# Second weight matrix fetched one load sooner, wider fillers, a counted instruction fetch, and the last product copied and stored by token halves

## The chip, the cores and the metric

The kernel runs on one core of one Trainium2 chip. A core has five engines that run side by side and meet at semaphores: TensorE (PE in the profile; its weight loads are shown apart as PEld), VectorE (DVE), ScalarE (ACT), GpSimd (POOL) and SyncE (SP), and 16 DMA engines that move data between HBM and the on-chip memory. TensorE writes its results to PSUM, which has eight banks of 128 x 512 float32; VectorE and ScalarE carry them from there to the on-chip memory SBUF. The metric is the device time of one execution in microseconds. Three runs of the kernel before took 301.09, 302.47 and 301.96 us, with a median of 301.96 us.

## The reference

Retention (attention with a decay in place of a softmax) for 8 batches, 8 heads, 576 positions and 64 features per head, then a feed-forward layer over all 4,608 tokens:

```python
scale = 1.0 / np.sqrt(64)
scores = scale * np.matmul(q, k.transpose(0, 1, 3, 2))
gamma = 1.0 - 2.0 ** (-5.0 - np.arange(H))
rel = pos[:, None] - pos[None, :]
Dmat = np.where(rel >= 0, gamma[:, None, None] ** rel[None, :, :], 0.0)
attn_out = np.matmul(scores * Dmat[None], v)
x = attn_out.transpose(0, 2, 1, 3).reshape(B * S, 512)
h = x @ w_in                 # 512 -> 2048
g = h * np.cos(h)
out = g @ w_out              # 2048 -> 512, float32
```

All inputs are float32; the kernel multiplies in bfloat16 and sums in float32.

## The kernel before, in words

**Retention by units.** A unit is (batch, g): g = 0 and 1 are the two blocks of 256 positions, g = 2 the remaining 64 positions of four batches together. `unit` (L468) loads k, q and v of a unit on SyncE (`load`, L457), and casts and scales them, k (`natk`) by a plain cast on GpSimd at L454, q and v (`qnat`, `natv`) by a multiplication with the decay tables at L496, also on GpSimd. For the first units k and q are transposed on TensorE (`tpe`, L509), for the later ones by a DMA (`txb`, L528). `scores` (L565) makes q·k on TensorE and the masked copy `pt` on VectorE (L599); the running state k·v is summed in the banks `st`; `outputs` (L637) makes pt·v plus state·q, and ScalarE copies the result to `xt`, the left operand of the feed-forward layer. All of these small products have line L563 in the profile.

**Feed-forward by tiles.** Nine tiles of 512 tokens. `mlp1` (L727) makes one 128-row slice of h with four matmuls (L737), ScalarE makes cos(h) (L745) and VectorE the product `gt` (L748). For the first tiles it is done by halves of 256 tokens. The second product of tile 0 is plain (`plain2`, L767: sixteen groups of four matmuls of 512 columns, L776; group `qd` needs quarter `qd` of `w_out`). Tiles 1 to 8 use a Winograd form with seven products of half size (`wino2`, L805, order P1, P2, P6, P5, P7, P3, P4; L862), whose sums of `gt` (`s`, L823 and L829) and of `w_out` (`tw`, `wsums`, L802) are made on VectorE. Products that go into the output are copied by ScalarE (`snap`), or added by VectorE (`comb`, L874), into `os`, and `store` (L753) writes `os` to HBM from SyncE. The last tile holds the 64-position ends of all batches, so its rows go out as two stores of 64 partitions each.

**What sets the order.** Every operation is a task with an estimated duration. `Graph.run` (L204) places the tasks one after the other, engine by engine, by due times (`prio`), free PSUM banks and its own estimate of when an operand is there; the order so found is then written out as a fixed instruction stream for each engine. Waits are semaphores; every engine executes its own stream strictly in order. The estimates matter through the order alone. Three of them are touched here: `dma_free` (L294), when a transfer gets the DMA engines; `FETCH` with `left` (L134, L208, L237, L280), a model of TensorE's instruction fetch, which comes in blocks of 256 instructions; and `count`, how many instructions a TensorE task has.

**Loads of the weights.** `load_w` (L715) issues the four quarters of a weight matrix on GpSimd's own queue with a cast to bfloat16; `graph` (L902) gates them: w_in waits for the load of k of unit (1,0), w_out (L940) for the load of v of unit (1,1). The loads of unit (2,0), on SyncE's queue, wait for quarter 1 of w_out (L943); SyncE's later loads stand behind them.

**Fillers.** Where the plan leaves TensorE idle for more than 400 ns before the bank of `self.wb` is given back, `emit` (L383) puts in matmuls of ones by ones, 128 columns each (L401), whose result nobody reads.

**The end.** In the last tile P3's sum is stored first, then P4: sixteen matmuls into one bank, one copy on ScalarE, two stores of 64 partitions by 2 x 256 columns.

## Time and profile before

| | |
|---|---|
| median of three runs | 301.96 us |
| the profiled execution: its own time / its span | 301.62 us / 299.9 us |
| TensorE busy | 285.2 us, 95% of the span |
| VectorE / ScalarE / GpSimd busy | 213.0 / 169.7 / 101.4 us |
| TensorE clock granted | 1.00 over the span |
| moved by DMA | 49.87 MB, mean 166 GB/s |
| instruction fetch (queue q8) | 30 packets, 0.49 MB |

The span runs from the first to the last instruction of the profiled execution; 1.7 us of its time lie outside. A row of the timeline has the start, the duration, the engine, the line, the operation, what it writes and reads, how many instructions are merged, and in brackets the idle time before it with what ended it. The duration of a merged row ends with the last instruction. "issue" stands for idle time in which the engine waited for no semaphore. The table by windows has, for each stretch, its length and each engine's busy time with the number of instructions, then the granted clock, the busy share of the DMA engines and their GB/s. A DMA instruction of SP or POOL is shown while it is being issued; its data land later.

### The profile page before, as it was taken

Reading aid. Unit: us, or ns where it says so; the run is one execution under the profiler, and the core shown is the slowest. Engines: PE = TensorE matmul, PEld = TensorE weight load, DVE = VectorE, ACT = ScalarE, POOL = GpSimd, SP = SyncE. Lnnn points to the kernel's source line nnn. Section 1 sums busy time; section 2 is a strip of 40 time slices with the busy share of each in tenths; the row PEclk is TensorE's granted clock in tenths of the full one; section 3 lists DMA queues with packets and bytes.
Section 4 is the critical chain, followed back from the end, with each engine's and each line's share of the span. In section 5 each row is a group of like instructions: output and inputs, shape, how many; then the busy total and the mean of one; then the engine's idle time right before and its main releaser. Section 6 shows DMA issues by size and latency. Waiting matters only on the chain.

```text
span 299.9 us, 9086 instructions
## 1 busy us (share of the span) xinstructions
PE 285.2 (95%) x3809; PEld 202.7 (68%) x3815; DVE 213.0 (71%) x379; ACT 169.7 (57%) x315; POOL 101.4 (34%) x125
## 2 busy tenths in 40 slices
PE   6789888999999999999999999999999999999994
PEld 6667665666788876766676667666766666666683
DVE  2776495659985889697868686959777666667721
ACT  5369876556667565645655565466565555545420
POOL 3821960665825614825363515172100000000000
PEclk9999999999999999999999999999999999999999
DMA  7999789999999799997999986892103000300115
GB/s 199 252 203 274 202 129 236 280 200 299 207 251 297 151 194 281 214 227 210 229 280 232 244 188 94 194 236 53 24 2 140 2 2 2 140 2 0 70 73 140
DMA packets 101640, 49.87 MB, mean 166 GB/s; under 512 B 43488, under 2 KB 97248, under 8 KB 101600
## 3 DMA queue, kind: packets, MB, share of 16 engines
q1 hardware_dynamic: 97376, 45.10, 63.6%
q0 software_dynamic: 4224, 4.19, 8.8%
q8 instruction: 30, 0.49, 0.7%
q14 instruction: 10, 0.08, 0.1%
HBM read 36.70 MB, written 9.44 MB: 154 GB/s over the span
## 4 chain that ended last, share of the span: by engine, by line
PE 78%; DMA 14%; POOL 5%; issue 1%; SPq 0%; ACT 0%; DVE 0%; DVEq 0%
PE bk L737 35%; PE bk L862 33%; DMA stgq<-in_q_dram 8%; PE bk L563 6%; DMA wout<-in_moe_w_out_dram 3%; DMA win<-in_moe_w_in_dram 3%; PE bk L776 2%; POOL qnat L496 2%; POOL natv L496 2%; PE st L563 1%; POOL natk L454 1%; SPq L463 0%; POOL win L717 0%; POOL wout L721 0%; DVE qnat L496 0%
## 5 line engine op out<-in xcount | busy, mean ns | idle before, releaser
L745 ACT ACTIVATE cb<-bk,cpi 128x256 bf16<-128x256 f32 (+1 forms) x192 | 108.3, 583 | 82.0 <-PE bk L737 79.9
L737 PE MATMUL bk<-xt,win 128*128 128x256 bf16 (+1 forms) x768 | 144.2, 326 | 1.0 <-DMA win<-in_moe_w_in_dram 0.7
L748 DVE TENSOR_TENSOR gt<-bk,cb 128x256 bf16<-128x256 f32 (+1 forms) x192 | 103.8, 555 | 54.9 <-ACT cb L745 47.8
L737 PEld LDWEIGHTS bk<-xt,win 128*128 128x128 bf16 x768 | 72.3, 98 | 39.7 <-DVE pt L599 1.4
L496 POOL TENSOR_TENSOR natv<-stgv,wv 128x512 bf16<-128x512 f32 x36 | 37.7, 1070 | 37.0 <-PE bk L563 20.6
L599 DVE TENSOR_TENSOR pt<-bk,tr 128x512 bf16<-128x512 f32 x68 | 42.7, 682 | 5.5 <-PE bk L563 5.4
L496 POOL TENSOR_TENSOR qnat<-stgq,wq 128x512 bf16<-128x512 f32 x32 | 35.0, 1112 | 15.9 <-DMA stgq<-in_q_dram 15.3
L454 POOL CAST natk<-stgk 128x512 bf16<-128x512 f32 x34 | 21.3, 653 | 55.8 <-DMA stgk<-in_k_dram 44.8
L862 PE MATMUL bk<-wout,gt 128*128 128x256 bf16 x256 | 32.7, 273 | 0.0
L862 PE MATMUL bk<-tw,s 128*128 128x256 bf16 x256 | 32.7, 273 | 0.0
L862 PE MATMUL bk<-wout,s 128*128 128x256 bf16 x256 | 32.4, 273 | 0.0
L862 PEld LDWEIGHTS bk<-tw,s 128*128 128x128 bf16 x256 | 24.9, 98 | 8.1
L862 PEld LDWEIGHTS bk<-wout,gt 128*128 128x128 bf16 x256 | 24.7, 98 | 6.4
L862 PEld LDWEIGHTS bk<-wout,s 128*128 128x128 bf16 x256 | 24.7, 98 | 6.1
L453 ACT ACTIVATE xt<-bk 128x512 bf16<-128x512 f32 x36 | 23.5, 728 | 0.5 <-PE bk L563 0.5
L874 DVE TENSOR_TENSOR os<-bk,sn 128x512 f32<-128x512 f32 x24 | 16.4, 683 | 10.4 <-PE bk L862 10.4
L453 ACT ACTIVATE sn<-bk 128x512 f32<-128x512 f32 x24 | 14.3, 597 | 13.8 <-PE bk L862 13.8
L862 PE MATMUL bk<-tw,gt 128*128 128x256 bf16 x128 | 16.4, 273 | 0.0
L776 PE MATMUL bk<-wout,gt 128*128 128x512 bf16 x58 | 15.3, 380 | 0.6 <-issue 0.3
L862 PEld LDWEIGHTS bk<-tw,gt 128*128 128x128 bf16 x128 | 12.5, 98 | 4.0
L829 DVE TENSOR_TENSOR s<-gt 128x1024 bf16<-128x1024 bf16 x16 | 12.8, 800 | 0.2
L563 PE MATMUL bk<-qt,kt 64*64 64x128 bf16 (+1 forms) x576 | 12.1, 217 | 0.4 <-ACT xt L453 0.4
(58 smaller groups left out, 187.7 us busy)
## 6 DMA issues: line engine op xcount, KB each, us to landing
stgk<-in_k_dram SPq DMA_DIRECT2D x16, 512.0 KB, 7.0
stgq<-in_q_dram SPq DMA_DIRECT2D x16, 512.0 KB, 6.9
stgv<-in_v_dram SPq DMA_DIRECT2D x16, 512.0 KB, 6.9
out_dram<-os SPq DMA_DIRECT2D x16, 512.0 KB, 3.3
win<-in_moe_w_in_dram POOLq DMA_DIRECT2D x4, 512.0 KB, 9.0
wout<-in_moe_w_out_dram POOLq DMA_DIRECT2D x4, 512.0 KB, 10.0
stgk<-in_k_dram SPq DMA_DIRECT2D x8, 128.0 KB, 3.4
stgq<-in_q_dram SPq DMA_DIRECT2D x8, 128.0 KB, 3.5
```

The costliest lines, as they stand in the source:

```text
L453: return self.one(eng, dur, lambda e: e.activation(dst(), src(), AF.Copy), r=r, w=w, **kw)
L454: return self.one(eng, dur, lambda e: e.tensor_copy(dst(), src()), r=r, w=w, port=True, **kw)
L496: self.one(eng, 610 if eng == "dve" else 1000, lambda e, out=out, inp=inp, tab=tab, col=col, hs=hs: e.tensor_tensor(out(), inp(), ap(tab, ...
L563: return lambda e: e.matmul(out(), lhs(), rhs(), start=start, stop=True, skip_group_check=True)
L599: self.one("dve", 610, lambda e, r=r, b=b, pt=pt: e.tensor_tensor(ap(self.at(pt), 1024, 0, 128, 512 * r, [64 * ny * ny, 8 // ny // ny], [1 ...
L737: inst = e.matmul(ap(self.at(bk), 512, 0, 128, 0, [1, n]), ap(self.WIN, 4 * DFF, 0, 128, c * DFF + 128 * f, [1, 128]), ap(self.at(xt), 204 ...
L745: self.one("act", 70 + n, lambda e: e.activation(ap(self.at(cb), TB, 0, 128, 0, [1, n]), ap(self.at(bk), 512, 0, 128, 0, [1, n]), AF.Sin, ...
L748: self.one("dve", 75 + n / 0.96, lambda e: e.tensor_tensor(ap(self.at(gt), NF * TB, 0, 128, f * TB + 256 * h0, [1, n]), ap(self.at(bk), 51 ...
L776: inst = e.matmul(self.at(bk).ap(), ap(self.at(gt), NF * TB, 0, 128, f * TB + 256 * half + 128 * tt, [1, 128]), ap(self.WOUT, NF * DM, 0, ...
L829: self.one("dve", 610, lambda e, i=i, q=q, x=x, y=y, op=op: e.tensor_tensor(sv(i, q), x(), y(), op), r=r, w=[(S_[i, q],)], port=True, name ...
L862: inst = e.matmul(ap(self.at(bank), 512, 0, 128, 256 * tt, [1, 256]), l(f, tt), rr(f), start=(first and f == 0 and tt == 0), stop=True, sk ...
L874: self.one("dve", 610, lambda e: e.tensor_tensor(view(h, c), ap(self.at(bank), 512, 0, 128, 0, [256, 2], [1, 256]), ap(self.at(sn[name]), ...
```

## The change

Five edits in one:

1. `graph`: the quarters of w_out are gated by the load of q of unit (1,1), not of v, which is the next one on SyncE's queue. On GpSimd the four issues now stand ahead of the two multiplications that make `qnat` of unit (1,1), where they stood behind them. The loads of unit (2,0) wait for quarter 2 of w_out, where they waited for quarter 1.
2. `warm`: a filler is one matmul of 512 columns in place of 128, and there are fewer of them: 24 where there were 103. The sixth place (one filler) is the last; the five fillers within the scores of unit (1,1) are gone.
3. The planner counts TensorE's instructions (8.4 for four matmuls, 16.4 for eight, fillers too) and asks for block k at instruction 128 + 256 k, which it expects 6,500 ns later, when instruction 443 + 256 k needs it. `dma_free` charges a GpSimd transfer 2,400 ns rather than 1,700 ns where the queue would be empty.
4. In the last tile bank A becomes two banks, one for each 128 tokens. P4's two tasks are by tokens (all eight slices of one half, then of the other) rather than by slices. Copies and sums from A come in two halves of 128 x 256.
5. The last store of 64 x 2 x 256 in two instructions becomes 64 x 256 in four, two after each half's copy, all on SyncE.

Since the order is planned, edits 1 and 3 also change it: the `tpe` of q of unit (1,1) now stand behind the outputs of unit (0,1); four groups of `plain2` (two with quarter 0, two with quarter 1) stand ahead of and between the two halves of the scores of unit (1,1), which come later; and VectorE has the first two weight sums (`tw`, from quarters 0 and 1) ahead of the `pt` copies of unit (1,1). The states of unit (2,0) on TensorE now have nineteen `mlp1` groups of tile 1 behind them, where sixteen stood behind them. From tile 2 on, a few tasks change places.

```diff
-    AHEAD, FETCH = 2000, 3000
+    AHEAD, FETCH = 2000, 6500
...
+    def fill(gap, seen):
+        return int(0.6 * (gap - 150) / 220 if seen else (gap - 300) / 430)
...
-                if e == "pe" and t.count > left[0]:
-                    s = max(s, left[1] - t.dur * left[0] / t.count)
+                if e == "pe" and t.count:
+                    k = (seen + t.count - 443) // 256
+                    if k >= 0 and 443 + 256 * k > seen and k in asked:
+                        s = max(s, asked[k] + self.FETCH - t.dur * (443 + 256 * k - seen) / t.count)
...
+                if gap > 400 and s < 45000:
+                    seen += 2 * self.fill(gap, seen)
+                k = (seen + t.count - 128) // 256
+                if k >= 0 and k not in asked:
+                    asked[k] = s + t.dur * max(0, 128 + 256 * k - seen) / max(1, t.count)
+                seen += t.count
...
-                dma_free = max(dma_free, s + (1700 if e == "pool" else 1150)) + t.dma
+                dma_free = max(dma_free, s + (2400 if e == "pool" and s > dma_free - 700 else 1700 if e == "pool" else 1150)) + t.dma
...
-                    self.warm(int((gap - 300) / 110 if not warm else 0.6 * (gap - 150) / 57))
+                    self.warm(max(1, self.G.fill(gap, warm)))
...
-                inst = e.matmul(ap(self.at(self.wb), 512, 0, 128, 0, [1, 128]), self.ONE.ap(), self.ONE.ap(),
+                inst = e.matmul(self.at(self.wb).ap(), self.ONE.ap(), ap(self.ONE, 128, 0, 128, 0, [0, 4], [1, 128]),
...
-        A, Bb, C = Buf("bk"), Buf("bk"), Buf("bk")
+        last = j == NTB - 1
+        A, Bb, C = [Buf("bk") for _ in range(1 + last)], [Buf("bk")], [Buf("bk")]
...
+            halves = last and p == 4
             for q in range(2):
+                def mm(e, l=l, rr=rr, bank=bank, first=first, q=q, halves=halves):
+                    for f in range(8) if halves else range(4 * q, 4 * q + 4):
+                        for tt in (q,) if halves else range(2):
+                            inst = e.matmul(place(bank, tt), l(f, tt), rr(f), stop=True, skip_group_check=True,
...
             def comb(h, c, bank, name):
+                for i, b in enumerate(bank):
+                    self.one("dve", 610 // len(bank), lambda e, i=i, b=b: e.tensor_tensor(
...
-                if j == NTB - 1:
+                for i, b in enumerate(A):
+                    self.copy("act", 490 // len(A), lambda i=i: view(1, 0, i, len(A)), lambda b=b: flat(self.at(b), 0, len(A)),
+                              [(b,)], [(os[1], 0, x) for x in (range(2) if len(A) == 1 else (i,))])
+                if last:
                     self.store(j, 1, os[1], (256, 512))
-                    self.store(j, 1, os[1], (0, 256))
+                    for i in range(2):
+                        self.store(j, 1, os[1], (0, 256), (i,))
...
-        gate = [(st["v", (1, 1)], 0)]
+        gate = [(st["q", (1, 1)], 0)]
         for x in range(4):
             self.load_w("wout", x, gate, 200 + x)
-        self.unit((2, 0), gate=[("wout", 1, 0)])
+        self.unit((2, 0), gate=[("wout", 2, 0)])
```

## The prediction

> **What bounds the kernel now.** I read the page's first line, then the table by windows to see where TensorE isn't full, then TensorE's timeline there, then the DMA queues and the end.
>
> ```profile
> PE 285.2 (95%) x3809; PEld 202.7 (68%) x3815; DVE 213.0 (71%) x379; ACT 169.7 (57%) x315; POOL 101.4 (34%) x125
> ...
> 34.10:40.80 6.70, 6.39 (x160) 5.00 (x163) 6.16 (x15) 5.79 (x14) 6.70 (x9) 1.00 0.48 99
> 40.80:47.10 6.30, 4.63 (x117) 2.99 (x108) 4.08 (x9) 3.38 (x7) 1.45 (x2) 1.00 1.14 178
> 47.10:60.40 13.30, 12.39 (x103) 8.11 (x105) 8.27 (x18) 8.35 (x18) 5.26 (x7) 1.00 1.16 262
> ...
> 61.00:282.00 221.00, 220.56 (x2851) 151.91 (x2853) 169.89 (x279) 125.89 (x224) 71.48 (x77) 1.00 0.68 155
> ```
>
> TensorE is the bound: between 61 and 282 us it is idle for 0.44 of 221 us. The same matmuls run there after the change, so only what comes before 61 us and after the last matmul can move the time.
>
> ```profile
> 15.95 0.73 PE L401 MATMUL bk<-one 128*128 128x128 bf16 x10 [0.46 <-issue]
> 31.14 0.40 PE L517 MATMUL bk<-idn,qnat 128*128 128x128 bf16 x4 [1.13 <-POOL qnat L496]
> ...
> 41.11 0.45 PE L401 MATMUL bk<-one 128*128 128x128 bf16 x5
> 41.93 0.42 PE L563 MATMUL bk<-qt,kt 64*64 64x128 bf16 x16 [0.36 <-ACT xt L453]
> ...
> 47.10 0.24 PE L563 MATMUL bk<-qt,sba 64*64 64x128 bf16 x1 [1.04 <-issue]
> 60.41 0.44 PE L563 MATMUL st<-natv,natk 64*64 64x64 bf16 x16 [0.66 <-POOL natv L496]
> ```
>
> Two idle times end without a semaphore, in the middle of equal matmuls: instruction fetch. Counting two instructions per matmul from the start, they fall near instructions 444 and 1,467, 1,023 apart, which is four blocks of 256. The first is spent in fillers and absorbed by the 1.13 us wait at 31.14; the second is in the open. From 34.1 us to 61 TensorE loses 0.16 + 0.45 (fillers) + 0.36 + 0.18 + 1.04 + 0.66 = 2.85 us. The last of these waits for v of unit (2,0), whose load stands behind w_out. GpSimd's timeline, and the DMA queues from 47.1 to 50.4 us (packets, MB, share of the engines):
>
> ```profile
> 37.16 3.03 POOL L721 DMA_DIRECT2D wout<-in_moe_w_out_dram  x4
> 58.32 2.04 POOL L496 TENSOR_TENSOR natv<-stgv,wv 128x512 bf16<-128x512 f32 x2
> ```
> ```profile
> q0 software_dynamic: 660, 0.65, 123.0%
> q1 hardware_dynamic: 18, 0.01, 1.1%
> ```
>
> From 36.40 to 38.40 us the same table by windows shows a DMA share of 0.00: the engines wait for w_out. Then w_out (q0) holds them alone until 50.4 us, though SyncE issued unit (2,0) (q1) from 47.06 us. At the end:
>
> ```profile
> 293.81 1.91 PE L862 MATMUL bk<-tw,gt 128*128 128x256 bf16 x16
> 294.73 0.59 SPq L761 DMA_DIRECT2D out_dram<-os  x1
> 295.37 0.61 SPq L761 DMA_DIRECT2D out_dram<-os  x1
> 295.76 0.60 ACT L453 ACTIVATE os<-bk 128x512 f32<-128x512 f32 x1 [4.64 <-PE bk L862]
> 296.38 0.60 SPq L761 DMA_DIRECT2D out_dram<-os  x1
> 297.02 0.67 SPq L761 DMA_DIRECT2D out_dram<-os  x1
> ```
>
> The last store is issued at 297.02 and lands 2.6 us later. SyncE needs 0.64 us from one such issue to the next and is idle for only 0.40 us before 296.38.
>
> **The change part by part**, against the profiled execution (301.62 us, 0.34 below the median of 301.96; its span is 299.9).
>
> *Fillers.* 103 of 128 columns become 24 of 512. Together the old ones show 8.4 us, all but the last five ahead of 31 us, in waits for loads. The first 37 take 3.59 us from 1.12 on; nine wide ones, at 0.22 us each in the rows of L776 and up to 1.7 times that so early (97 ns for each of the 37, 57 to 66 later), end no later, and the next real matmul, at 5.74, waits for GpSimd in any case. I take 0: the cover is the wait of 1.13 us at 31.14; without it a filler in the way would cost at most its own 0.22 us. The clock row is 1.00 throughout.
>
> *w_out sooner.* GpSimd ends natk of unit (1,1) at 35.20, and q had landed, for qnat began at 35.16 without a wait. So the four issues start at 35.2 and not 37.16: 1.96 us sooner, into the idle DMA. Its quarters landed at 42.95 (issue plus the 5.8 us of the shortest), 47.07, 49.62 and 52.61 (VectorE's waits end there); now 41.0, 45.1, 47.7, 50.65. Bounds for the shift: 0, if v's tail takes the room, to 2.0; I take 1.96, since v was down by 36.4 when the first packets of w_out, 1.2 us after issue, would come. qnat of (1,1) moves back by 3.03 us, to 40.3.
>
> *TensorE up to the states of (2,0).* Outputs (0,1) began at 39.81; without two `tpe`, but with banks held by `pt` and `gt` copies, I take 39.6 to 40.55. Then, by rows: `tpe` 0.24, group of quarter 0 at 41.0 (waits 0.2), `tpe`, group, until 43.0; `mlp1` waits for `xt` and the scores for `qt`, 0.25 together, as ScalarE's four copies follow at 0.6 us each; states until 44.5; quarter 1 at 45.1 (0.6). VectorE stands in the same wait: `tw` (0.69) and one `pt` (0.62) come before the next free bank at 46.5, so TensorE waits 0.45 more; quarter 3 costs 0.2. With the 0.35 before 39.6 that is 2.1 us lost by 52.9; before, 2.2 of the 2.85 were lost by 60. Then outputs (1,1) 1.1, seven `mlp1` groups 3.1, one `plain2` 0.87: the states are reached at about 58.2.
>
> *v of unit (2,0).* Its loads wait for quarter 2: 47.7, against 47.06. A store issued at 292.99 moved first data at 294.3, so a free queue needs 1.3 us: 49.0. The DMA is free of w_out at 48.4. Before, they began at 50.4: 1.4 to 1.5 us sooner, so natv is ready at 58.9, not 60.36, and TensorE waits there until 58.9. But three more `mlp1` groups (1.31 us) are left behind this point. Front: 1.31 - 1.5 = **-0.2 us**. Bounds: +1.8 (natv 0.5 later, as the gate is), and -0.9 (TensorE on time at 58.2). The wait of 1.04 goes, but what is late next is natv, so its gain isn't added.
>
> *Fetch.* With 79 filler matmuls fewer the blocks are needed at other places than the two stalls. Asked-to-running took 7.7 and 7.1 us in the two stalls (8.28 to 15.95, 39.96 to 47.10, counting to instruction 128 of each block). The closest pair I count in the new order, 315 instructions around 66 to 74 us, takes 8.3 us at the rows' durations. I take 0; up to 1.0 if that block is slow.
>
> The Trainium skill (Runtime: NRT & Kernel Launch, "Instruction fetch mechanics") says that the fetch is mostly hidden, as the sequencer issues more slowly than blocks arrive. The row of 1.04 us speaks against it; by the page rival C falls away and the sum stays.
>
> *The end.* P4 by halves has the same sixteen matmuls. The halved sums and copies (128x256: 0.42 on VectorE, 0.38 on ScalarE) lengthen os by 0.15, hidden as SyncE's first pair ends at 294.33 and its next begins at 294.73; uncovered it would add 0.15. The first half's copy ends near 295.2, the last's near 296.15, 0.2 sooner. But SyncE has six issues from 294.73 on, not four: the last starts at 294.73 + 5 x 0.64 = 297.93 and lands 2.4 later (the shortest landing of such a store), at 300.3, not 299.6: **+0.7 us**. Bounds: with the 0.37 us of a store of 128 partitions (258.12 us) per small issue the copies set the end, -0.3; with the 0.72 from 292.99 to 293.71 and 2.6 to land, +1.3. I take 0.64, the rows of 64 partitions being the nearest.
>
> Sum: -0.2 + 0.7 = +0.5: 302.1 in the profiled execution, **302.5** beside the median. The last matmul ends near 295.5, the span near 300.4.
>
> **The rivals** (on the median). 0.5%, 1.5 us, is about what a measurement of this kernel can tell from no change: 300.45 to 303.47.
>
> B, slower: the loads of (2,0) don't profit. If q1 has to share from its issue, the later gate counts and not the free DMA; natv comes as before: +1.31 + 0.7 = +2.0, **304.0**. It decides when natv is less than 0.5 us sooner. Against it: 18 packets of q1 beside 660. The Trainium skill (DMA: Bandwidth & Descriptors, "Queues, rings and completion order") has each engine go round robin between its queues; by that rule B would hold. The trace disagrees.
>
> C, a fetch stall: one of the blocks near 70 us late by 1.0: **303.5**.
>
> D, splitting pays: small issues cost 0.37, so the end gives 0.3: **301.5**. For it: ScalarE is done 0.2 sooner and half the bytes are left. Against it: every store of 64 partitions costs 0.6. The Trainium skill (Perfetto Trace Analysis, "DMA Optimizations") says that splitting may end a task sooner where the DMA engines are idle; they are, but here SyncE isn't.
>
> E, faster: all 2.85 us go, if natv is there by 57.6 and the quarters hold nobody up: -2.85 + 0.7, **299.8**. Against it: TensorE can't pass quarter 1 before 45.1.
>
> That the weights don't start sooner is B with another cause.
>
> **How the numbers follow.** Forecast 0.50 (its own range 301.6 to 303.4), B 0.18, C 0.11, D 0.13, E 0.08. The range of 300.6 to 304.2 leaves out E and B's upper half. Faster by over 0.5%: E, a little of D and of the forecast, 0.13. Slower: B, half of C, 0.08 of the forecast, 0.30. Within: 0.57.
>
> **What would show it.** w_out issued at 35.2 us and no empty DMA behind it; natv of (2,0) done near 58.9 and a short wait of the states for it; no "issue" of 1 us on TensorE; VectorE waiting for quarter 1 near 45; the last matmul near 295.5; six issues of SyncE without a gap from 294.5 to 298.4. I am wrong if natv comes as before, if a wait for `pt` or a bank exceeds 1 us between 41 and 58, or if the small issues cost 0.4.

## The result, and the profile after

The changed kernel takes 303.72 us (median of 20 executions, 302.60 to 305.15); the kernel before, beside it on the same chip, 301.73 us (20 executions, 300.57 to 304.70). The ratio is 1.0062, with a 95% interval of 1.0042 to 1.0081: **slower by 0.62%**, 2.0 us. The execution profiled took 303.60 us with a span of 301.88; before, 301.62 and 299.90. So these two are 2.0 us apart as well, and the traces can be read against each other. Of several kernels here a part of the executions lies 2 to 4 us above the others; the ratios leave the most disturbed ones out.

The front came as forecast. The lines of the page and of the table by windows that answer to those shown of before:

```profile
PE 287.5 (95%) x3736; PEld 198.0 (66%) x3736; DVE 212.7 (70%) x380; ACT 169.1 (56%) x318; POOL 100.2 (33%) x125
...
34.10:40.80 6.70, 6.41 (x140) 4.33 (x128) 5.65 (x13) 4.89 (x13) 6.31 (x9) 1.00 0.72 126
40.80:47.10 6.30, 5.55 (x64) 2.90 (x64) 2.91 (x5) 3.57 (x7) 1.94 (x2) 1.00 1.19 195
47.10:60.40 13.30, 12.20 (x170) 8.19 (x170) 8.17 (x19) 8.08 (x19) 6.98 (x9) 1.00 1.26 241
61.00:282.00 221.00, 220.40 (x2847) 151.35 (x2846) 170.05 (x280) 124.92 (x224) 68.07 (x75) 1.00 0.68 155
```

From 40.8 to 47.1 us TensorE is busy for 5.55 us instead of 4.63, and the share of the DMA engines from 34.1 to 40.8 rose from 0.48 to 0.72. The last line holds a trap: 220.40 us of 221 busy, against 220.56 before, looks like the same work done equally well. It isn't, as is shown below.

TensorE's timeline, the rows with an idle time that ends in this stretch, and GpSimd's:

```profile
20.46 2.12 PE L746 MATMUL bk<-xt,win 128*128 128x256 bf16 x18 [0.61 <-issue]
29.40 0.39 PE L746 MATMUL bk<-xt,win 128*128 128x256 bf16 x2 [0.25 <-issue]
...
41.26 1.02 PE L785 MATMUL bk<-wout,gt 128*128 128x512 bf16 x4 [0.50 <-DMA wout<-in_moe_w_out_dram]
45.68 0.61 PE L746 MATMUL bk<-xt,win 128*128 128x256 bf16 x4 [0.29 <-DVE pt L608]
58.69 0.44 PE L572 MATMUL st<-natv,natk 64*64 64x64 bf16 x16 [1.01 <-POOL natv L505]
```
```profile
35.16 3.03 POOL L730 DMA_DIRECT2D wout<-in_moe_w_out_dram  x4 [0.39 <-DMA stgq<-in_q_dram]
38.18 2.09 POOL L505 TENSOR_TENSOR qnat<-stgq,wq 128x512 bf16<-128x512 f32 x2
...
56.60 2.04 POOL L505 TENSOR_TENSOR natv<-stgv,wv 128x512 bf16<-128x512 f32 x2
```

w_out is issued at 35.16 us, 2.00 sooner. The stall of 1.04 us at 47.1 is gone; two of 0.61 and 0.25 us stand earlier, ahead of waits for loads that swallow them. natv of unit (2,0) is done at 58.63 (60.36 before), and TensorE, which waits 1.01 us for it, begins the unit's states at 58.69, 1.72 us sooner. The DMA queues from 47.1 to 50.4 us (packets, MB, share of the engines) show why: w_out has half as much left there, and the loads on q1 move.

```profile
q0 software_dynamic: 311, 0.30, 55.3%
q1 hardware_dynamic: 773, 0.40, 42.3%
```

The end, from the timeline of all engines (a merged row's duration ends with its last instruction):

```profile
293.80 6.31 SPq L770 DMA_DIRECT2D out_dram<-os  x8
...
294.56 1.91 PE L876 MATMUL bk<-tw,gt 128*128 128x256 bf16 x16
...
295.64 0.38 ACT L462 ACTIVATE os<-bk 128x256 f32<-128x256 f32 x1 [3.77 <-PE bk L876]
296.51 0.38 ACT L462 ACTIVATE os<-bk 128x256 f32<-128x256 f32 x1 [0.49 <-PE bk L876]
```

SyncE issues eight stores without a gap, from 293.80 to 300.11 us; ScalarE's last copy is over at 296.89, and SyncE is 3.2 us behind it. The span ends 5.40 us behind the last matmul (296.47); before, 4.18 us behind 295.73.

Where the 2.0 us lie is seen by taking the same place of both traces. From 900 matmuls before the last one TensorE's order is the same in both, and at the other places of the table the same matmuls, in another order, are still to come, so "2,100 matmuls before the last one" is the same place:

| | before | after | after minus before |
|---|---|---|---|
| states of (2,0) begin | 60.41 | 58.69 | -1.72, with 1.31 us of work more behind it |
| 2,100 matmuls before the last | 118.20 | 118.21 | 0.01 |
| 1,800 before the last | 140.99 | 141.21 | 0.22 |
| 900 before the last | 207.72 | 208.47 | 0.75 |
| last matmul ends | 295.73 | 296.47 | 0.74 |
| span ends | 299.90 | 301.88 | 1.98 |

At the states the changed kernel is 1.72 - 1.31 = 0.41 us ahead; 60 us later that is gone; at 208 us it is 0.75 behind, and the end adds 1.2. The loss behind the states is 0.42 + 0.21 + 0.53 = 1.16 us, in a stretch that has hardly an idle TensorE. These are two single executions; the other profiles tell which of the three terms belongs to the order. The experiments below give seven traces with the new order of TensorE, this one among them, and six with the old one, that of before among them:

- From 1,200 to 900 matmuls before the last (0.53): 21.8 us in all seven with the new order, 21.2 in all six with the old one. This is the order's.
- From 2,100 to 1,800 (0.21): 23.00 us in this trace and 22.8 in the other twelve. This is of this execution alone.
- From the states to 2,100 before the last (0.42): with the new order 57.5 to 59.6 us less the 1.31 of more work, with the old one 57.7 to 60.9. Executions of one order differ by 2 to 3 us here, so the 0.42 can't be put down to the order.

The order of the whole kernel has 86 changes between full matmuls and the small ones on 64 x 64 lanes, against 82; all four more stand ahead of the place 2,100 before the last. That they cost something there isn't shown. At a change to lanes the weight loads stand idle for about 0.3 us, but they overlap the matmuls: from the start of four full matmuls to that of the scores behind them TensorE takes 0.96 us (199.30 to 200.26 in before), from four full ones to full ones 0.86 (204.32 to 205.18), 0.1 us less.

Most of the 0.53 us, 0.44, is lost at 202 us. TensorE's and VectorE's timelines there, of before and of after:

```profile
200.26 0.64 PE L563 MATMUL bk<-qt,kt 64*64 64x128 bf16 x32
200.83 1.05 PE L862 MATMUL bk<-wout,gt 128*128 128x256 bf16 x8
201.72 1.89 PE L737 MATMUL bk<-xt,win 128*128 128x512 bf16 x8
...
199.27 0.69 DVE L823 TENSOR_TENSOR s<-gt 128x1024 bf16<-128x1024 bf16 x1
...
201.34 0.68 DVE L748 TENSOR_TENSOR gt<-bk,cb 128x512 bf16<-128x512 f32 x1
```
```profile
200.57 0.64 PE L572 MATMUL bk<-qt,kt 64*64 64x128 bf16 x32
201.14 1.05 PE L876 MATMUL bk<-wout,gt 128*128 128x256 bf16 x8
202.47 1.89 PE L746 MATMUL bk<-xt,win 128*128 128x512 bf16 x8 [0.28 <-DVE gt L757]
...
199.58 0.69 DVE L832 TENSOR_TENSOR s<-gt 128x1024 bf16<-128x1024 bf16 x1
200.31 0.69 DVE L832 TENSOR_TENSOR s<-s,gt 128x1024 bf16<-128x1024 bf16 x1
201.03 0.69 DVE L838 TENSOR_TENSOR s<-gt,s 128x1024 bf16<-128x1024 bf16 x1
201.64 0.68 DVE L757 TENSOR_TENSOR gt<-bk,cb 128x512 bf16<-128x512 f32 x1
```

TensorE does the same three groups in both. In the new order VectorE has three sums `s` in a row ahead of the product `gt` that frees a bank, where before it has one, so the last group starts 1.33 us behind the one ahead of it and not 0.89. The same wait of 0.28 to 0.33 us at 201 to 205 us is in each of the seven traces with the new order, and in none of the six with the old one.

### The profile page after: what moved, and what is told of

The parts are those of the page before. It is cut to its first block, busy times and chain, and to the rows that moved or that the text cites. A ratio compares the mean times of both kernels' runs of the same rounds, so it can differ in the third digit from the quotient of the medians.

```text
span 301.9 us, 8931 instructions
## 1 busy us (share of the span) xinstructions
PE 287.5 (95%) x3736; PEld 198.0 (66%) x3736; DVE 212.7 (70%) x380; ACT 169.1 (56%) x318; POOL 100.2 (33%) x125
## 4 chain that ended last, share of the span: by engine, by line
PE 79%; DMA 12%; POOL 3%; DVE 2%; issue 1%; ACT 1%; SPq 0%; DVEq 0%
PE bk L746 37%; PE bk L876 32%; PE bk L572 6%; DMA stgq<-in_q_dram 6%; DMA wout<-in_moe_w_out_dram 4%; PE bk L785 2%; DMA win<-in_moe_w_in_dram 2%; PE st L572 1%; POOL natv L505 1%; DVE gt L757 1%; POOL qnat L505 1%; POOL wout L730 1%; DVE s L832 0%; SPq L472 0%; DVE qnat L505 0%
## 5 line engine op out<-in xcount | busy, mean ns | idle before, releaser
L746 PEld LDWEIGHTS bk<-xt,win 128*128 128x128 bf16 x768 | 71.4, 98 | 42.3 <-DVE pt L608 2.5
L505 POOL TENSOR_TENSOR natv<-stgv,wv 128x512 bf16<-128x512 f32 x36 | 38.6, 1095 | 31.3 <-PE bk L572 19.5
L463 POOL CAST natk<-stgk 128x512 bf16<-128x512 f32 x34 | 20.4, 626 | 61.1 <-DMA stgk<-in_k_dram 38.9
L505 POOL TENSOR_TENSOR qnat<-stgq,wq 128x512 bf16<-128x512 f32 x32 | 33.9, 1080 | 17.5 <-DMA stgq<-in_q_dram 17.5
L896 DVE TENSOR_TENSOR os<-bk,sn 128x512 f32<-128x512 f32 (+1 forms) x25 | 16.5, 662 | 12.8 <-PE bk L876 12.8
L462 ACT ACTIVATE sn<-bk 128x512 f32<-128x512 f32 (+1 forms) x26 | 14.5, 565 | 12.8 <-PE bk L876 12.8
L785 PE MATMUL bk<-wout,gt 128*128 128x512 bf16 x64 | 16.5, 380 | 0.5 <-DMA wout<-in_moe_w_out_dram 0.5
L876 PE MATMUL bk<-tw,gt 128*128 128x256 bf16 x128 | 16.4, 273 | 0.0
L572 PEld LDWEIGHTS bk<-qt,kt 64*64 64x64 bf16 x576 | 8.9, 106 | 7.0 <-issue 4.7
```

The lines of the kernel that those rows point to most:

```text
L462: return self.one(eng, dur, lambda e: e.activation(dst(), src(), AF.Copy), r=r, w=w, **kw)
L463: return self.one(eng, dur, lambda e: e.tensor_copy(dst(), src()), r=r, w=w, port=True, **kw)
L505: self.one(eng, 610 if eng == "dve" else 1000, lambda e, out=out, inp=inp, tab=tab, col=col, hs=hs: e.tensor_tensor(out(), inp(), ap(tab, ...
L572: return lambda e: e.matmul(out(), lhs(), rhs(), start=start, stop=True, skip_group_check=True)
L746: inst = e.matmul(ap(self.at(bk), 512, 0, 128, 0, [1, n]), ap(self.WIN, 4 * DFF, 0, 128, c * DFF + 128 * f, [1, 128]), ap(self.at(xt), 204 ...
L785: inst = e.matmul(self.at(bk).ap(), ap(self.at(gt), NF * TB, 0, 128, f * TB + 256 * half + 128 * tt, [1, 128]), ap(self.WOUT, NF * DM, 0, ...
```

## The experiments

Each execution was timed beside executions of the kernel before on the same chip; its median there was 301.80, 301.43, 302.11 and 301.82 us in the four batches. "Tail" is the time from the end of the last matmul to the end of the span. All parts that an experiment doesn't name are those of the kernel it starts from.

### The end: which part of it costs

The end alone, on the kernel before:

```diff
+        last = j == NTB - 1
+        A, Bb, C = [Buf("bk") for _ in range(1 + last)], [Buf("bk")], [Buf("bk")]
...
+                    for i in range(2):
+                        self.store(j, 1, os[1], (0, 256), (i,))
```

> The kernel before with edits 4 and 5 alone: two banks and halved copies, and four stores of 64 x 256 in place of two of 64 x 2 x 256. The orders of TensorE and GpSimd are those of before. Theory 1 (SyncE's two more issues set the end): the last matmul ends as before (295.7 us in the profile), the span ends 5.0 to 5.4 us behind it, where it was 4.2, so the time is 0.7 to 1.3 us above before; the last six issues stand without a gap. Theory 2 (the end costs nothing by itself, and the long issue of 1.32 us seen in the changed kernel was chance): span 4.2 us behind the last matmul, time as before.

302.29 us, ratio 1.0026 (0.9985 to 1.0066). The tail is 4.97 us, and the last six issues stand without a gap, as theory 1 has it. The time is 0.5 us up by the medians, under its 0.7 to 1.3, and by the ratio it is no change that can be measured. The last matmul isn't as before, but at 298.76 us: the profile came from a high execution (the last section).

The changed kernel with the old end:

```diff
-        last = j == NTB - 1
+        last = False
...
-                    for i in range(2):
-                        self.store(j, 1, os[1], (0, 256), (i,))
+                    self.store(j, 1, os[1], (0, 256))
```

> The changed kernel with edits 4 and 5 undone, so edits 1 to 3 alone: the end is that of before. Theory 1: the span ends 4.2 us behind the last matmul, which ends near 296.5 us as in the changed kernel (295.7 before), so the time is 0.5 to 0.9 us above before and 1.0 to 1.3 below the changed kernel. Theory 2: all of the 2 us stay, +1.9 us against before. Theory 3 (the first part gains, as 1.72 us at the states of unit (2,0) less 1.31 us of work suggest, and the rest of the 0.75 us is chance): -0.4 us against before.

302.77 us, ratio 1.0028 (0.9996 to 1.0060). The tail is 4.16 us, that of before. Theory 1 has this tail, but not the place of the rest: the last matmul ends at 295.82 us, 0.09 behind before where 0.8 was expected, and of the 0.97 us between the medians some 0.6 lie outside the span (the last section).

The changed kernel with the sums and copies by halves, but two stores and not four:

```diff
-                    for i in range(2):
-                        self.store(j, 1, os[1], (0, 256), (i,))
+                    self.store(j, 1, os[1], (0, 256))
```

> The changed kernel with its last store in two instructions of 64 x 2 x 256 again, behind the second half's copy; banks and copies stay halved. Theory 1: two issues fewer, so the end is 0.8 to 1.2 us sooner than in the changed kernel: span some 4.0 to 4.3 us behind the last matmul. Rival (the halved sums on VectorE and copies delay SyncE's first pair, and this moves all that follows): no change against the changed kernel, 5.4 us behind the last matmul.

302.94 us, ratio 1.0022 (0.9988 to 1.0056). The tail is 4.17 us. So the halves of the sums and copies cost the tail nothing and bring it nothing; it is the two stores more. They cost 4.97 - 4.18 = 0.8 us of tail in one order and 5.40 - 4.17 = 1.2 in the other, and in time 303.72 - 302.94 = 0.8 us.

The kernel before with its last store issued by ScalarE, to see whether SyncE's issues set the end there too:

```diff
-                    self.store(j, 1, os[1], (0, 256))
+                    self.store(j, 1, os[1], (0, 256), ("sp", "act"))
```

> The kernel before with the second of its two last stores issued by ScalarE, right behind the copy, beside the first on SyncE. Theory 1 (the issues in a row on SyncE are what the end waits for): both issues start near 296.4 us, the last lands 0.4 to 0.7 us sooner, time 0.3 to 0.7 us below before. Rival (the transfers themselves or their landing set the end): no change.

301.65 us, ratio 0.9989 (0.9943 to 1.0035). The last two issues began at 296.02 and 296.03 us, side by side; the last of before began at 297.02, and yet the tail is 4.44 us: the last issue began 0.66 us behind the last matmul, 0.63 sooner than in before, and the end came 0.26 later. So in before it isn't the last issue that sets the end, as the rival has it. The table by windows (busy time of PE, PEld, DVE, ACT and POOL, the clock, the share of the DMA engines, GB/s), for before, for this kernel and for the changed one:

```profile
296.00:298.00 2.00, 0.00 (x0) 0.00 (x0) 0.00 (x0) 0.36 (x1) 0.00 (x0) 1.00 0.97 235
```
```profile
296.00:298.00 2.00, 0.00 (x0) 0.00 (x0) 0.00 (x0) 0.00 (x0) 0.00 (x0) 1.00 0.90 220
```
```profile
296.00:298.00 2.00, 0.47 (x5) 0.18 (x2) 0.00 (x0) 0.40 (x2) 0.00 (x0) 1.00 0.71 160
298.00:300.00 2.00, 0.00 (x0) 0.00 (x0) 0.00 (x0) 0.00 (x0) 0.00 (x0) 0.98 0.84 235
300.00:302.00 2.00, 0.00 (x0) 0.00 (x0) 0.00 (x0) 0.00 (x0) 0.00 (x0) 0.50 0.27 66
```

In before and in this kernel the DMA engines are busy for 0.97 and 0.90 of these two microseconds. That they are the limit there is a reading, and not shown: the share reaches 1.26 elsewhere (47.1 to 60.4 us). In the changed kernel they are at 0.71, and in the last two microseconds at 0.27, waiting for SyncE. By this reading the end has two limits close together, 1.05 MB of stores and SyncE's row of issues, and the split moved it from the one to the other.

The second limit is tested by giving two of the four last stores of the changed kernel to ScalarE:

```diff
-                        self.store(j, 1, os[1], (0, 256), (i,))
+                        self.store(j, 1, os[1], (0, 256), (i,), ("sp", "act"))
```

> The changed kernel, with the four last stores (64 x 256 each) shared out: two issued by SyncE, two by ScalarE, the first of these ahead of ScalarE's last copy. Transfers, copies and the order of TensorE are those of the changed kernel. Theory (SyncE's eight issues in a row are the end's loss): SyncE issues six, so the span ends 4.2 to 4.6 us behind the last matmul instead of 5.40, and the time is 302.5 to 303.1 us, 0.7 to 1.2 below the changed kernel's 303.72. Rival (four transfers of 64 KB end later than two of 128 KB, whoever issues them): 5.1 to 5.5 us behind the last matmul, 303.5 us or more.

303.43 us, ratio 1.0059 (1.0039 to 1.0080). The tail is 4.37 us, as the theory has it; the time is not, being 0.3 above its range. SyncE's and ScalarE's rows:

```profile
293.00 5.06 SPq L770 DMA_DIRECT2D out_dram<-os  x6
```
```profile
294.84 0.38 ACT L462 ACTIVATE os<-bk 128x256 f32<-128x256 f32 x1 [3.77 <-PE bk L876]
295.25 0.54 ACTq L770 DMA_DIRECT2D out_dram<-os  x1
295.84 0.38 ACT L462 ACTIVATE os<-bk 128x256 f32<-128x256 f32 x1 [0.62 <-PE bk L876]
296.25 0.49 ACTq L770 DMA_DIRECT2D out_dram<-os  x1
```

As its profile came from its lowest execution (301.92 us), the same kernel was taken again:

> The split of the last four stores over SyncE and ScalarE once more: its first profile had the end of theory (4.37 us behind the last matmul), but its median of 303.43 us was hardly below the changed kernel's, and that profile came from its lowest execution. Theory (the end is mended in every execution, and the front made the difference): 4.2 to 4.6 us behind the last matmul again, and what the time has above 302 lies ahead of the last matmul, in waits of TensorE between 0 and 120 us. Rival (the first profile was a lucky end): 4.9 us or more behind the last matmul, with SyncE's or ScalarE's issues longer than 0.9 us each.

302.92 us, ratio 1.0027 (0.9997 to 1.0057), tail 4.76 us: between the two expectations. SyncE's second issue took 1.30 us this time and its last 1.23; one of 1.32 us is in the changed kernel's profile too. Over all 24 executions the median is 303.14 us, 0.6 below the changed kernel; the two ratios are 1.0059 and 1.0027, the changed kernel's 1.0062. With SyncE relieved of two issues 1.03 and 0.64 of the 1.22 us that the tail had lost are back, and that confirms the cause; why a single issue takes 1.2 to 1.3 us now and then stays open. The Trainium skill (Perfetto Trace Analysis, "DMA Optimizations") advises to balance transfers over the engines that can issue them where the issuing engine looks busy and the DMA engines don't; the tails of 4.37 and 4.76 against 5.40 agree with it, and on the kernel before, where the DMA engines look busy, 4.44 against 4.18 agrees with its condition.

### The front: which part of it costs

The first edit alone, on the kernel before:

```diff
-        gate = [(st["v", (1, 1)], 0)]
+        gate = [(st["q", (1, 1)], 0)]
...
-        self.unit((2, 0), gate=[("wout", 1, 0)])
+        self.unit((2, 0), gate=[("wout", 2, 0)])
```

> The kernel before with the first edit alone: the second weights' four loads wait for unit (1,1)'s q instead of its v, and the loads behind them for quarter 2 instead of quarter 1. Fillers, planner and end are those of before. The planned order of TensorE's matmuls, fillers left out, is then the same as in the changed kernel, group for group. Theory (the order costs): the front of the changed kernel loses about 1 us of median against before, and the order, with four more switches between full matmuls and 64x64 lanes, is the reason; then this run lies where the changed front with the old end lay, 302.4 to 303.2 us, natv of (2,0) done near 58.2 to 58.6 us. Rival (the fillers and the fetches cost): the wide fillers let the code fetches be asked for later, and that is the loss; then this run lies at 301.5 to 302.0 us, with natv as early.

302.68 us, ratio 1.0033 (1.0013 to 1.0054); natv of (2,0) done at 57.90 us. The edit does what it says, sooner than forecast even, and the kernel is 1.0 us slower by the ratio, 1.25 by the medians. That is in the theory's range; that the switches are the reason isn't shown by it. Of the kernels with the changed front and the old end this is the one whose interval leaves out no change.

The wide fillers alone:

```diff
-                inst = e.matmul(ap(self.at(self.wb), 512, 0, 128, 0, [1, 128]), self.ONE.ap(), self.ONE.ap(),
+                inst = e.matmul(self.at(self.wb).ap(), self.ONE.ap(), ap(self.ONE, 128, 0, 128, 0, [0, 4], [1, 128]),
```

> The kernel before with the second edit alone: 25 fillers of 512 columns in place of 103 of 128; every other instruction stands in the order of before, and the end is that of before. Theory (the order costs): no change beyond 0.3 us, 301.4 to 302.0 us, the last matmul ends at 295.4 to 296.0 us; code fetches of the first three blocks are asked for 2 to 4 us later, since 78 matmuls fewer stand ahead of them, and any stall falls into a wait for loads. Rival (the fillers and the fetches cost): 302.3 to 303.0 us, with waits of TensorE of 0.5 us or more that nothing but the fetch explains, between 15 and 60 us.

302.01 us, ratio 1.0010 (0.9985 to 1.0034), the last matmul at 295.88 us. The theory's range misses it by 0.01; by the ratio it is no change. What the 0.6 us between the medians are is told in the last section. The trace has stalls of 1.14 and 0.26 us that end without a semaphore at 20.45 and 29.41 us, where the changed kernel has its two, and not the 1.04 us at 47.1: the fillers moved them.

The planner alone (its count of instructions, the fetch latency of 6.5 in place of 3.0 us, the charge for GpSimd's transfers):

```diff
-    AHEAD, FETCH = 2000, 3000
+    AHEAD, FETCH = 2000, 6500
...
-                if e == "pe" and t.count > left[0]:
-                    s = max(s, left[1] - t.dur * left[0] / t.count)
+                if e == "pe" and t.count:
+                    k = (seen + t.count - 443) // 256
+                    if k >= 0 and 443 + 256 * k > seen and k in asked:
+                        s = max(s, asked[k] + self.FETCH - t.dur * (443 + 256 * k - seen) / t.count)
```

> The kernel before with the third edit alone: the planner's model of the code fetches (instructions counted, latency 6.5 in place of 3.0 us) and its charge for GpSimd's transfers; fillers, gates and end are those of before. TensorE's order is a third one: 8 more groups than before, two more switches to or from lanes; the loads are issued as in before, so that natv of (2,0) is done at 60.0 to 60.6 us. Theory (the order costs, by its switches): between before and the changed front, 301.8 to 302.8 us. Rival (a planner that knows the fetches better takes stalls away): 300.8 to 301.5 us, and no wait near 46 us that only the fetch explains (1.04 us in before).

305.90 us, ratio 1.0144 (1.0119 to 1.0168), the slowest order of all; both expectations fall. Its waits of TensorE have a line of 3.4 us that before hasn't:

```profile
PE bk L746 <- DVE gt L757: 3.4, 6, 1.6
```

The counting took no stall away that mattered (TensorE still loses 1.20 us at 45.3), and the new order runs into VectorE six times. In the changed kernel this order isn't used: the first edit alone already gives the changed kernel's order of TensorE, fillers left out, group for group. So the new planner has no effect on TensorE's order there.

The first edit consists of sooner transfers and of the order that the planner makes from them. They can be taken apart: plan with one pair of gates, then move the four issues, and swap the gates, in the finished plan. First the old order with the sooner transfers:

```diff
         order = self.G.run(None)
+        # the four w_out issues: ahead of qnat of (1,1), waiting for q; loads of (2,0): on quarter 2
+        order = [t for t in order if t not in sooner]
+        at = next(i for i, t in enumerate(order) if t.eng == "pool" and any((q11, 0) in p[2] for p in t.parts))
+        order[at:at] = sooner
```

> The kernel before with the transfers of the first edit alone: planned with the old gates, so that TensorE's order is that of before group for group, and then, behind the planner, the four w_out issues stand ahead of the two q scalings of unit (1,1) on GpSimd and wait for its q, and the loads of (2,0) wait for quarter 2. Theory (the sooner loads are good by themselves, the new order is what costs): natv of (2,0) done at 58.0 to 58.8 us, the wait of 0.66 us ahead of its states gone, the last matmul 0.3 to 0.7 us sooner than in before on its undisturbed trace (295.0 to 295.5), and a median of 300.9 to 301.5 us, 0.2 to 0.7 below before's. Rival (the sooner loads cost, by what they do to other transfers and to the code fetches): 302.3 us or more.

305.16 us, ratio 1.0097 (1.0068 to 1.0125). natv was done at 58.45 us as expected, and the theory falls all the same: the sooner loads aren't good by themselves. The rival had named other reasons. TensorE's timeline and GpSimd's say which:

```profile
39.13 0.38 PE L531 MATMUL bk<-idn,qnat 128*128 128x128 bf16 x4 [3.07 <-POOL qnat L510]
```
```profile
34.86 3.04 POOL L735 DMA_DIRECT2D wout<-in_moe_w_out_dram  x4
37.88 2.10 POOL L510 TENSOR_TENSOR qnat<-stgq,wq 128x512 bf16<-128x512 f32 x2
```

The four issues take GpSimd 3.04 us. In the old place they stand behind qnat of unit (1,1); ahead of it they delay it by just that, and in the old order TensorE transposes it at once.

The same with the wide fillers:

```diff
-                    self.warm(int((gap - 300) / 110 if not warm else 0.6 * (gap - 150) / 57))
+                    self.warm(max(1, self.G.fill(gap, warm)))
```

> As the run before it, with the 25 fillers of 512 columns in place of 103 of 128. TensorE's order, fillers left out, is that of before. Theory (fillers are worth nothing by themselves): within 0.4 us of the run with narrow fillers, 300.9 to 301.8 us. Rival (fewer fillers move the blocks of the code so that stalls of 1 us come more seldom or more often): a median 0.5 us or more from it, with the wait near 46 us that only the fetch explains (1.04 us in before) gone or doubled.

304.67 us, ratio 1.0097 (1.0065 to 1.0130). That is 0.49 us below the run with narrow fillers, between the 0.4 of the theory and the 0.5 of the rival, and both runs are far above the theory's range, for the reason just given. Here TensorE idled 3.24 us for qnat, and its clock fell to half behind it. The table by windows of this run and of the one before it:

```profile
39.80:43.20 3.40, 3.40 (x33) 2.48 (x32) 2.04 (x4) 2.16 (x5) 2.19 (x3) 0.50 1.06 157
```
```profile
39.80:43.20 3.40, 3.37 (x86) 2.57 (x86) 2.81 (x7) 3.02 (x7) 2.17 (x3) 1.00 1.15 184
```

Sixteen `mlp1` matmuls take 3.06 us in the first (from 40.90) and 2.12 in the second (from 40.46). The Trainium skill (TensorE: Matmul & The Clock Gate, "What's actually happening") puts the idle window after which the clock is halved at about 3.4 us, on a grid that doesn't start with the kernel. The stretch at half clock, 3.4 us long, agrees with such a window. The idle time is a little shorter than it, and the measurement decides: 3.24 us were enough in this execution, 3.07 in the other weren't.

The reverse, the new order with the old transfers:

```diff
         order = self.G.run(None)
+        # the four w_out issues: behind qnat of (1,1), waiting for v; loads of (2,0): on quarter 1
```

> The reverse: planned with the first edit, so that TensorE's order is that of the changed kernel, and then the w_out issues put back behind the two q scalings on GpSimd, waiting for v, and the loads of (2,0) put back on quarter 1. Narrow fillers, old end. Theory (the order is bought by the loads, which it needs): natv of (2,0) done at 60.0 to 60.6 us, TensorE waits 2 to 3 us ahead of its states (0.7 with the sooner loads), and the median is 304.0 to 305.3 us, 1.5 to 2.5 above the run with both. Rival (sooner loads cost as much as they bring): 302.3 to 303.2 us, the median of the run with both.

304.50 us, ratio 1.0081 (1.0055 to 1.0107); natv at 60.03 us. The time is the theory's; the place isn't. The wait came 17 us ahead of the states, at the quarters of w_out, and the states then waited for nothing:

```profile
43.32 1.02 PE L795 MATMUL bk<-wout,gt 128*128 128x512 bf16 x4 [2.35 <-DMA wout<-in_moe_w_out_dram]
47.15 1.04 PE L795 MATMUL bk<-wout,gt 128*128 128x512 bf16 x4 [0.69 <-DMA wout<-in_moe_w_out_dram]
```

The four cells, as ratios to before:

| | old transfers | sooner transfers |
|---|---|---|
| old order | 1 | 1.0097 |
| new order | 1.0081 | 1.0033 (1.0013 to 1.0054) |

Each half of the first edit without the other costs 0.8 to 1.0%; together they cost 0.3%. The planner did what it had to for the new place of the issues: it moved work to where qnat is late. The order so found has the loss of 0.53 us ahead of 208 us, in every trace, and it alone is more than the 0.41 us that the changed kernel won at the states. What else the front loses lies between 58 and 119 us and changes from one execution to the next (the last section). No kernel here beats the kernel before by what can be measured.

## Why the prediction was right or wrong

The time, 303.72 us, lies in the range and 1.2 us above the forecast of 302.5. The likeliest class was "no change that can be measured", at 0.57; it is 0.62% slower, and slower had 0.30. The 0.5% that it set as its bound lies inside the interval.

**Right: the front up to the states of (2,0).** The issue of w_out (35.16 against 35.2 us), the cover of the fillers, the gone stall of 1.04 us, natv (58.63 against 58.9), TensorE waiting for it there, and the three groups of 1.31 us left behind it. Net -0.41 us; the text had -0.2, with natv as the next thing late. TensorE was at the states at 57.68 us, not 58.2, since the quarters of w_out and the banks held it up less than forecast (0.50 and 0.29 us); its wait of 1.01 us for natv hid that. That the 2.85 us of idle time ahead of 61 us could not be had (rival E) was right because natv was what came late next; for quarter 1, named against E, TensorE did not wait.

**Wrong: what comes after that.** The step that failed is the sentence that the same matmuls run from 61 us on, so that only the time before and the end can move. The matmuls are the same, their order isn't, and the text costed the new order only up to the states of (2,0). What the runs showed in its place: 1.16 us lost between 59 and 208 us in this execution, of which 0.53 us, most of it at the wait for VectorE at 202 us, stand in every trace with the new order and in none with the old one. The other 0.63 us are not shown to be the order's. The row from 61 to 282 us gave no warning, as the idle time in it grew only from 0.44 to 0.60 us: most of a loss of this kind counts as busy. By the ratios the kernels with the changed front and the old stores are 0.7 to 1.0 us slower than before (1.0028, 1.0022 and 1.0033, only the last clear of no change), by the medians 1.0 to 1.25, where the text had 0.2 us faster.

**Wrong in size: the end.** The mechanism was right: eight issues in a row set the end, not the copies, and the loss is that of two issues. Its term was 0.7 us, and 1.22 were measured, inside its bound of 1.3. The last issue began 3.04 us behind the last matmul, and 1.29 before, so 1.75 later and not 0.91: the issues came 0.72 us apart, not 0.64, and the first of the six had to wait for an issue of 1.32 us. The landing took 2.06 us, not 2.4, which gave 0.3 back. The DMA engines, which the text called idle at the end, are busy for 0.97 of the time from 296 to 298 us of before.

**The rivals.** B gave 304.0 us and C 303.5, near the time, and neither is what happened: natv came 1.73 us sooner (B), and no fetch stall shows near 70 us (C). D fell: SyncE's small issues took 0.60 to 0.90 us each and not 0.37, and the end alone isn't faster (1.0026). That the new order might be slower behind the states was in no rival; the planner alone found one that costs 1.4%. The time stayed within the range although a loss was put at nothing: the range was wide enough for it, but not made for it.

## What to carry to other kernels

An order that is written out ahead has no local edits: a gate moved by one load re-sorted TensorE's work as far as 208 us, and half a microsecond was lost at the far end of it. Compare the whole order, by which engine each group comes to wait for, and align the two traces from the end. Do it with several traces of each order: a difference of one pair can belong to the execution. Before an issue is moved ahead of compute on the same engine, price the issues themselves: four took GpSimd 3.04 us, and in the old order TensorE paid all of it. Before a last store is split, look at how busy the DMA engines and the issuing engine are just ahead of the last landing; here the first looked full, and the split made it the second.

## What was not expected of the hardware

**A code fetch may end the execution.** The time outside the span (known to 0.05 us, as the spans are) was 1.68 to 1.80 us in all 52 undisturbed executions of the tested kernels with narrow fillers, and 1.68 to 3.28 us in the 86 of those with wide fillers, above 1.85 in 48 of them. The DMA queues in the last microseconds, of the changed front with the old end (wide fillers, 2.53 us outside) and of the first edit alone (narrow, 1.72 us):

```profile
q1 hardware_dynamic: 480, 0.59, 34.4%
q8 instruction: 1, 0.02, 1.1%
```
```profile
q1 hardware_dynamic: 502, 0.64, 38.5%
```

In the first, TensorE's last block of code starts to arrive at 301.77 us, when the span has been over since 299.98 and nothing is left to run, and it lands at 302.82; in the profile of the wide fillers alone, at 301.87 and 303.20. 78 or 79 matmuls fewer, two instructions each, have moved the boundaries of the blocks of 256 so that the last block is asked for at the very end. In the changed kernel's profile that block landed at 295.45, so the profile doesn't show this cost; over its 20 executions the mean outside the span is 1.92 us against 1.73 for narrow fillers. For the wide fillers alone it is 2.22, which is most of what their median is above before. This was read from the traces; padding the code to move the boundary back was not tried. Counted from the start of the span, both blocks land 0.31 us behind the end of the execution's own time (302.51 and 302.89 us), so what exactly the end waits for is open.

**One of the high executions has two more fetch stalls.** The profile of the end alone (305.45 us, 3.2 above that kernel's median) has two stalls that the others of the old order lack:

```profile
88.51 0.60 PE L742 MATMUL bk<-xt,win 128*128 128x256 bf16 x4 [0.87 <-ACT cb L750]
...
95.86 0.37 PE L568 MATMUL st<-natv,natk 64*64 64x64 bf16 x21 [0.84 <-issue]
```

By counting instructions, both fall where a block of code was due; those blocks took 10.0 and 10.2 us from the ask to the landing, against 8.2 and 6.0 in the trace with the last store on ScalarE, which has the same order. The first is put down to ScalarE in the row, though the time fits the fetch. Whether all the high executions of the kernel before have this cause was not shown. The Trainium skill (Runtime: NRT & Kernel Launch, "Instruction fetch mechanics"), by which the fetch is mostly hidden, holds for most blocks here, but not for these.

**VectorE's sums take longer beside GpSimd's work.** In the trace of before 54 of VectorE's operations of 128x1024 run with no GpSimd work beside them, and each takes 0.68 or 0.69 us; twelve that lie mostly beside GpSimd's casts and multiplications take 0.76 to 1.42. The front with split copies and the old stores has this where TensorE then waits 1.33 us for VectorE, at 72.8 us; the one with the old end has the same order there and no such wait. VectorE and GpSimd in the first and in the second:

```profile
70.45 1.42 DVE L832 TENSOR_TENSOR s<-s,gt 128x1024 bf16<-128x1024 bf16 x1
71.90 1.42 DVE L838 TENSOR_TENSOR s<-gt,s 128x1024 bf16<-128x1024 bf16 x1
...
69.84 2.94 POOL L505 TENSOR_TENSOR qnat<-stgq,wq 128x512 bf16<-128x512 f32 x2
```
```profile
71.20 0.98 DVE L832 TENSOR_TENSOR s<-s,gt 128x1024 bf16<-128x1024 bf16 x1
72.22 0.69 DVE L838 TENSOR_TENSOR s<-gt,s 128x1024 bf16<-128x1024 bf16 x1
...
72.36 2.46 POOL L505 TENSOR_TENSOR qnat<-stgq,wq 128x512 bf16<-128x512 f32 x2 [0.72 <-DMA stgq<-in_q_dram]
```

The two sums are 1.17 us longer in the first. The first edit alone has the same at 79.45 and 80.82 us (1.45 and 1.53 us), and TensorE waits 0.67 us for VectorE at 82.8. So when the loads let GpSimd start, against VectorE's sums, makes part of what executions of one order differ by between 58 and 119 us. This was read from the traces and not tested by a run.

**Left open.** The changed front with split copies and the old stores had longer spans than the one with the old end (medians 301.15 and 300.30 us) and shorter times outside (1.74 and 2.50), so that the times are alike. How much of the front's loss stays when GpSimd and VectorE don't meet was not measured.
